# Building the two exponential tables of a 64-channel half jointly, in one tile

## The chip, the cores and the metric

The kernel runs on one core of one Trainium2 chip. The metric is the device time of one execution in microseconds (us), as the median of several runs on the same chip. A profile is one traced execution; its times count from the start of the span.

## The reference, cut to what matters

The program is four residual layers over x of 2048 x 512: A, B, A, B. Layer A is a state-space convolution, layer B a local dilated attention (not touched by the change).

```python
# layer A, on the layer-normalised input u (2048 x 512), D = 512 channels, N = 128 modes
dt = exp(log_dt)
P  = exp(dt * (A_re + 1j*A_im) [:, :, None] * l)      # D x N x 2048
K  = einsum("dn,dnl,dn->dl", Cc, P, dt*Bc).real       # the convolution kernel, D x 2048
y  = irfft(rfft(pad(u)) * rfft(pad(K)))[:2048] + u * Dskip
# ...
x = x + A(layernorm(x)); x = x + B(layernorm(x)); x = x + A(layernorm(x)); x = x + B(layernorm(x))
```

K depends on the parameters only, so the kernel builds it once, in its first stage, mixed with the first convolution. That stage is where the change lies.

## The kernel before

P at position l = 64*e + i is a product of a table X over e (32 entries) and a table Y over i (64 entries). The kernel works in eight halves of 64 channels. For each half DVE (VectorE) fills X and Y by doubling (entries m to 2m are entries 0 to m times a power), then makes three quarter products; PE (TensorE) contracts X with Y over the modes; ACT (ScalarE) evacuates the sum into KTq; a DMA takes it to DRAM and another fetches it in another layout as KT.

```python
def double(self, T, m, lev, hc):                       # before
    for e0 in range(0, m, HALF):                       # HALF = 8: pieces of at most 1024 columns
        mm = min(m, HALF)
        ta, tb = ...                                   # two scratch tiles
        nc.vector.tensor_tensor(v(ta), src, self.mult(self.MA, lev, hc, mm), ALU.mult)
        nc.vector.tensor_tensor(v(tb), src, self.mult(self.MB, lev, hc, mm), ALU.mult)
        nc.vector.tensor_tensor(T[..., m + e0:m + e0 + mm, :], ta, tb[:, ::-1], ALU.add)
# y_products: 3 x (Y quarter, Y2 quarter), each one tensor_tensor of 2048 columns
# contract: 256 small matmuls psk <- X, Y and psk <- X, Y2, then
        self.KTq = self.wk.tile([128, 1024], BF, name="KTq", tag="KTq")   # a buffer of its own
        nc.scalar.copy(KTq..., psk...)
        nc.sync.dma_start(self.kscr[hc]..., KTq...)
```

The first stage in program order. The input's FFT (`u_fft`), the kernel's spectrum (`k_fft`) and `finish` (spectral products, inverse, residual, write of X) are issued between tables and contraction.

```python
def half(hc, between=None):
    Xt, Y, Y2 = T.build(hc)
    T.x_part(Xt, hc); T.y_base(Y, hc); T.y_products(Y, Y2, hc)     # (half 0: y_base first)
    r = between() if between is not None else None     # u_fft(dc + 1) or k_fft(dc - 1)
    with tc.high_priority():
        T.contract(Xt, Y, Y2, hc)
    return r

for dc in range(4):                                    # a pair of halves = 128 channels
    Xr = residual(dc - 1) if dc > 0 else None
    Kt = half(dc * 2, (lambda: k_fft(dc - 1)) if dc > 0 else None)
    if dc > 0:
        cv.finish(dc - 1, xcs.pop(dc - 1), Kt, Xr)
    if dc < 3:
        half(dc * 2 + 1, mid)                          # mid: xcs[dc + 1] = cv.u_fft(dc + 1)
# ... half 7 in two parts, k_fft and finish of the last pair
```

`u_fft` and `k_fft` go matmuls (PE) - Z (ACT) - transposes (PE) - zt copy (DVE for the input, ACT for the kernel) - matmuls (PE) - xc or Kt (ACT). `finish` goes pa, pb (DVE) - inverse matmuls (PE) - VT (ACT) - matmuls with the residual Xr (PE) - X (ACT).

Of the kernel before, what the change touches and what calls it, by code (L numbers as in the profile page):

```python
# [19 lines left out]
D = 512  # L20
# [67 lines left out]

def make_consts(nc, const, C):
    fc = _fft_consts()  # L90
    bones_np = np.zeros((128, 4, 32), dtype=np.float32)
    for f in range(128):
        for k in range(4):
            bones_np[f, k, 8 * k + f // 16] = 1.0
    for name in ("F1", "F1T"):
        C[name + "_h"] = nc.inline_tensor(_bf(fc[name]), name="c_" + name)
    todo = [("ident", _bf(np.eye(128)), BF), ("C2", _bf(fc["C2"]), BF), ("IC", _bf(fc["IC"]), BF),
            ("bones", _bf(bones_np), BF), ("onesr", _bf(np.ones((1, 128))), BF)]
    for i, (name, arr, dt) in enumerate(todo):
        h = nc.inline_tensor(arr, name="c_" + name)  # L100
        t = const.tile(list(arr.shape), dt, name="sb_" + name)
        nc.sync.dma_start(t[:], h.ap())
        C[name] = t
# [32 lines left out]
class LnStats:  # L136


    def __init__(self, nc, pool, parts, nm, eps):
        self.nc, self.parts, self.eps = nc, parts, eps  # L140
        self.st = pool.tile([128, NJ, len(parts), 6], F32, name="ln_st_" + nm)
        self.mv = pool.tile([128, NJ, 2], F32, name="ln_mv_" + nm)
        self.den = pool.tile([128, NJ], BF, name="ln_den_" + nm)
        self.rstd = pool.tile([128, NJ], F32, name="ln_rstd_" + nm)
        self.nb = pool.tile([128, NJ], F32, name="ln_nb_" + nm)
# [208 lines left out]
def ladder(nc, pp, pst, identf, raw, MA, MB, cb, nu, fill):  # L354
# [27 lines left out]
    quad = pp.tile([128, 4, 4, NM], F32, name="quad")  # L382
    nc.vector.tensor_tensor(quad[:, :, 0, :], e[:], cs[:], ALU.mult)
    nc.vector.tensor_tensor(quad[:, :, 1, :], e[:], sn[:], ALU.mult)
    LAM = pp.tile([128, 2, D], F32, name="LAM0")
# [10 lines left out]
    def coefs():  # L396
# [12 lines left out]
        for q in (2, 3):  # L409
            pt = pst.tile([128, 4, NM], F32, name="ptq", tag="ptq")  # L410
            for t in range(4):
                nc.tensor.transpose(pt[:, t, :], quad[:, t, q, :], identf[:])
            nc.scalar.copy(cb[:, :, q - 2, :], pt[:].rearrange("n t (h d) -> n (t h) d", h=2))

    def multipliers(i, cur):

        src = cur[:].rearrange("n c (h d) -> n c h d", h=8)
        if i == "nu":
            nc.scalar.copy(nu[:, :, 0, :], src[:, 0])
            nc.scalar.activation(nu[:, :, 1, :], src[:, 1], ACT.Copy, scale=-1.0)  # L420
            return
        nc.scalar.copy(MA[:, i], src[:, 0].unsqueeze(2).to_broadcast([128, 8, 2, 64]))
        conj = 7 <= i <= 10
        nc.scalar.activation(MB[:, i, :, 0, :], src[:, 1], ACT.Copy, scale=-1.0 if conj else 1.0)
        nc.scalar.activation(MB[:, i, :, 1, :], src[:, 1], ACT.Copy, scale=1.0 if conj else -1.0)
# [3 lines left out]
    for i in range(11):  # L429
# [6 lines left out]
        multipliers(i if i != 6 else "nu", cur)  # L436
# [4 lines left out]
        if i == 5:  # L441
            l48 = pp.tile([128, 2, D], F32, name="l48")
            q1 = pp.tile([128, 2, D], F32, name="q1")
            q2 = pp.tile([128, 2, D], F32, name="q2")
            nc.vector.tensor_tensor(q1[:], l16[:], cur[:, 0:1, :].to_broadcast([128, 2, D]), ALU.mult)
            nc.vector.tensor_tensor(q2[:], l16[:], cur[:, 1:2, :].to_broadcast([128, 2, D]), ALU.mult)
            nc.vector.tensor_tensor(l48[:, 0, :], q1[:, 0, :], q2[:, 1, :], ALU.subtract)
            nc.vector.tensor_tensor(l48[:, 1, :], q1[:, 1, :], q2[:, 0, :], ALU.add)
            multipliers(LV48, l48)
# [5 lines left out]
class Tables:  # L455


    def __init__(self, nc, tc, es, MA, MB, cb, nu, psum, kscr):
        self.nc, self.MA, self.MB, self.cb, self.nu, self.ps, self.kscr = nc, MA, MB, cb, nu, psum, kscr
        self.tx = es.enter_context(tc.tile_pool(name="t_x", bufs=2))  # L460
# [3 lines left out]
    def mult(self, M, lev, hc, n):  # L464
        return (M[:, lev, hc].rearrange("n c (h t) -> n (c h) t", t=2).unsqueeze(2)
                .to_broadcast([128, 2 * HD, n, 2]))

    def double(self, T, m, lev, hc):

        nc = self.nc  # L470
        for e0 in range(0, m, HALF):
            mm = min(m, HALF)
            ta = self.wk.tile([128, 2, HD, HALF * 2], BF, name="ta", tag="ta")
            tb = self.wk.tile([128, 2, HD, HALF * 2], BF, name="tb", tag="tb")

            def v(t):
                return t[:].rearrange("n c h (e t) -> n (c h) e t", t=2)[:, :, 0:mm, :]
            src = T[:, :, :, e0:e0 + mm, :].rearrange("n c h e t -> n (c h) e t")
            nc.vector.tensor_tensor(v(ta), src, self.mult(self.MA, lev, hc, mm), ALU.mult)  # L479
            nc.vector.tensor_tensor(v(tb), src, self.mult(self.MB, lev, hc, mm), ALU.mult)  # L480
            nc.vector.tensor_tensor(T[:, :, :, m + e0:m + e0 + mm, :].rearrange("n c h e t -> n c h (e t)"),  # L481
                                    ta[:, :, :, 0:mm * 2], tb[:, ::-1, :, 0:mm * 2], ALU.add)

    def build(self, hc):
        nc = self.nc
        Y = self.ty.tile([128, 2, HD, EY, 2], BF, name="Ytab", tag="Ytab")
        Y2 = self.ty.tile([128, 2, HD, EY - EYB, 2], BF, name="Y2tab", tag="Y2tab")
        X = self.tx.tile([128, 2, HD, EX, 2], BF, name="Xtab", tag="Xtab")
        return X, Y, Y2

    def x_part(self, X, hc):
        nc = self.nc
        nc.gpsimd.memset(X[:, 0, :, 0, :], 1.0)
        nc.gpsimd.memset(X[:, 1, :, 0, :], 0.0)
        nc.vector.tensor_copy(X[:, :, :, 1, :].rearrange("n c h t -> n (c h) t"),
                              self.nu[:, hc].rearrange("n c (h t) -> n (c h) t", t=2))
        for lev in range(1, 5):
            self.double(X, 1 << lev, 6 + lev, hc)

    def y_base(self, Y, hc):  # L500
        self.nc.vector.tensor_copy(Y[:, :, :, 0, :].rearrange("n c h t -> n (c h) t"),
                                   self.cb[:, hc].rearrange("n c (h t) -> n (c h) t", t=2))
        for lev in range(4):
            self.double(Y, 1 << lev, lev, hc)

    def y_products(self, Y, Y2, hc, h0=0, h1=HD):

        nc = self.nc
        if h1 - h0 == HD:
            views = [(lambda t: t.rearrange("n c h e t -> n (c h) e t"), lambda m: m)]  # L510
        else:
            views = [(lambda t, c=c: t[:, c, h0:h1], lambda m, c=c: m[:, c * HD + h0:c * HD + h1]) for c in range(2)]
        for q, lev in ((1, 4), (2, 5), (3, LV48)):
            for v, vm in views:
                src = v(Y[:, :, :, 0:EYB, :])
                nc.vector.tensor_tensor(v(Y[:, :, :, q * EYB:(q + 1) * EYB, :]), src,  # L516
                                        vm(self.mult(self.MA, lev, hc, EYB)), ALU.mult)
                nc.vector.tensor_tensor(v(Y2[:, :, :, (q - 1) * EYB:q * EYB, :]), src,  # L518
                                        vm(self.mult(self.MB, lev, hc, EYB)), ALU.mult)

    def contract(self, X, Y, Y2, hc, half=None):
# [6 lines left out]
        for ds in range(n):  # L528
            for m in range(4):
                for g in range(4):  # L530
                    d = d0 + g * n + ds
                    h, t = d // 2, d % 2
                    xs = X[:, m // 2, h, :, t]
                    if m % 2 == 0:
                        nc.tensor.matmul(psk[32 * g:32 * g + 32, ds, :], xs, Y[:, m // 2, h, :, t],  # L535
                                         start=(m == 0), stop=False, skip_group_check=True)
                    else:
                        nc.tensor.matmul(psk[32 * g:32 * g + 32, ds, EYB:], xs, Y2[:, 1 - m // 2, h, :, t],  # L538
                                         start=False, stop=(m == 3), skip_group_check=True)
        if half != 1:  # L540
            self.KTq = self.wk.tile([128, 1024], BF, name="KTq", tag="KTq")
# [10 lines left out]
def kernel_and_first_conv(nc, tc, C, prm, x2d, const, kt_dram, kscr, ln, ln_b):  # L552
    with ExitStack() as es:
        mt = es.enter_context(tc.tile_pool(name="k_mt", bufs=1))
        MA = mt.tile([128, 11, 8, 2, 64], BF, name="MA")
        MB = mt.tile([128, 11, 8, 2, 64], BF, name="MB")
        cb = mt.tile([128, 8, 2, 64], BF, name="cb")
        nu = mt.tile([128, 8, 2, 64], BF, name="nu")
        psk = es.enter_context(tc.tile_pool(name="k_psk", bufs=1, space=PSUM))
        T = Tables(nc, tc, es, MA, MB, cb, nu, psk, kscr)  # L560
        with tc.tile_pool(name="k_prep", bufs=1) as pp, tc.tile_pool(name="k_pst", bufs=2, space=PSUM) as pst:
# [6 lines left out]
            Drow = mt.tile([1, D], BF, name="Drow")  # L568
            nc.sync.dma_start(Drow[:], prm["Dskip"].rearrange("(o d) -> o d", o=1))
# [10 lines left out]
            ladder(nc, pp, pst, identf, raw, MA, MB, cb, nu, fill)  # L580
        psT = es.enter_context(tc.tile_pool(name="k_psT", bufs=2, space=PSUM))
        psA = es.enter_context(tc.tile_pool(name="k_psA", bufs=2, space=PSUM))
        cv = Conv(nc, tc, es, C, X, psA, psT, ("zt_xc",))
# [3 lines left out]
        def half(hc, between=None):  # L587
            Xt, Y, Y2 = T.build(hc)
# [462 lines left out]
```

## Time and profile before

| | before |
|---|---|
| median, range (us) | 609.28 (609.2 to 611.79) |
| profiled span, mean granted TensorE clock | 606.0 us, 0.918 |
| last table product ends | 233.9 us |
| first X write of finish(0), (1), (2) | 127.2, 175.4, 225.4 us |
| first copy of the attention stage (xnT) | 266.3 us |

The page's list of busy time by engine, before (busy us, share of the span, number of instructions):

```profile
PE 445.1 (73%) x5743; PEld 289.0 (48%) x5786; DVE 514.4 (85%) x976; ACT 338.9 (56%) x465; POOL 12.7 (2%) x50
```

The view by windows, before (window, its length, then busy us and instructions of PE, PEld, DVE, ACT and POOL, then granted clock, DMA share and GB/s; PEld is PE's weight load):

```profile
195.00:245.00 50.00, 36.73 (x817) 27.16 (x820) 48.31 (x101) 29.30 (x38) 1.14 (x1) 0.88 0.20 55
```

DVE is busy 48.3 of 50 us: the stage runs at DVE's pace, and stays so up to 245 us. The groups by form, before, from 38 to 240 us (number, then total busy us and mean ns of one, then idle time before them), here one of the two groups of quarter products:

```profile
L516 DVE TENSOR_TENSOR Ytab<-Ytab,MA 128x2048 bf16<-128x2048 bf16 x21 | 25.6, 1220 | 0.2
```

### The profile page before, as it was taken

To read this page: it belongs to the slowest core of one execution; us is meant where nothing else is said; L and a number is where in the kernel's file an instruction comes from. 1 tells how busy PE (TensorE), PEld (TensorE's weight loads), DVE (VectorE), ACT (ScalarE), POOL (GpSimd) and SP (SyncE) were. 2 spreads that over 40 slices of the span, in tenths; PEclk is the share of its full clock that TensorE was granted. 3 is DMA by queue.
4 is the path that set the end of the run, shared out by engine and by line. 5 is a ranking of instruction groups with operands and counts; after the bars stand their busy time and mean duration, and the time that the engine had idled before them with its cause. 6 is when DMAs were issued, how large, how long until landed. Compare 5 with 4: busy or idle time off the path is not lost.

```text
span 606.0 us, 13365 instructions
## 1 busy us (share of the span) xinstructions
PE 445.1 (73%) x5743; PEld 289.0 (48%) x5786; DVE 514.4 (85%) x976; ACT 338.9 (56%) x465; POOL 12.7 (2%) x50
## 2 busy tenths in 40 slices
PE   1101776876767776679987779978995899858996
PEld 0100554564554565454332766656764433327763
DVE  5999799998998999775977899859999588689950
ACT  4999357555662755646574223467973556722144
POOL 0000000000000000400000000000000000000000
PEclk9999989898996897869998599989998799968999
DMA  9101001221131023600004060000000000040011
GB/s 291 67 1 35 19 20 37 87 56 36 41 103 37 3 106 72 209 1 1 2 1 118 4 264 16 2 0 1 3 1 0 2 2 0 1 121 1 1 72 69
DMA packets 24346, 28.78 MB, mean 47 GB/s; under 512 B 15074, under 2 KB 20067, under 8 KB 23007
## 3 DMA queue, kind: packets, MB, share of 16 engines
q1 hardware_dynamic: 22702, 27.54, 13.8%
q8 instruction: 45, 0.74, 0.5%
q10 hardware_dynamic: 1584, 0.39, 0.3%
q14 instruction: 15, 0.11, 0.1%
HBM read 15.89 MB, written 8.39 MB: 40 GB/s over the span
## 4 chain that ended last, share of the span: by engine, by line
DVE 52%; PE 28%; ACT 9%; issue 8%; DMA 2%; POOL 0%; SPq 0%; POOLq 0%; ACTq 0%; DVEq 0%
PE ps_qk L829 7%; DVE prod L931 6%; DVE ta L479 4%; DVE Y2tab L518 4%; DVE tb L480 4%; DVE Ytab L516 4%; PE ps_o L955 4%; PE ps_v L843 3%; DVE Xtab L481 3%; DVE ln_st_b L150 3%; PE Lp L875 2%; DVE Ytab L481 2%; PE po L946 2%; DVE ln_st_a L150 2%; DVE pa L726 2%
## 5 line engine op out<-in xcount | busy, mean ns | idle before, releaser
L946 PE MATMUL po<-sb_ident,prod 128*128 128x128 bf16 x1024 | 72.7, 232 | 11.4 <-DVE prod L931 7.9
L946 PEld LDWEIGHTS <-prod 128*128 128x128 bf16 x1024 | 65.2, 105 | 20.6 <-DVE prod L931 17.2
L829 PE MATMUL ps_qk<-xnT,wqk 128*128 128x512 bf16 x245 | 63.7, 391 | 4.3 <-ACT xnT L814 1.2
L862 DVE TENSOR_TENSOR prod<-qT,kT 128x2048 bf16<-128x2048 bf16 (+3 forms) x48 | 43.2, 953 | 14.0 <-ACT qT L831 7.2
L931 DVE TENSOR_TENSOR prod<-V,L 128x2048 bf16<-128x2048 bf16 (+3 forms) x48 | 43.6, 947 | 6.4 <-PE po L946 6.4
L949 ACT CAST oT<-po 128x1024 bf16<-128x1024 f32 x16 | 15.4, 1015 | 56.6 <-PE po L946 56.6
L195 PE MATMUL psA<-X,sb_F 128*128 128x128 bf16 x128 | 14.9, 236 | 36.2 <-ACT X L578 32.3
L870 DVE TENSOR_TENSOR prod<-qT,kT 128x2048 bf16<-128x2048 bf16 (+3 forms) x40 | 34.9, 902 | 6.9 <-ACT kT L831 4.3
L829 PEld LDWEIGHTS <-wqk 128*128 128x128 bf16 x256 | 23.5, 100 | 32.5 <-issue 12.2
L195 PEld LDWEIGHTS <-sb_F 128*128 128x128 bf16 x256 | 16.6, 100 | 45.6 <-issue 42.8
L535 PE MATMUL psk<-Ytab,Xtab 128*32 128x64 bf16 x1024 | 26.1, 214 | 15.6 <-DVE Xtab L481 5.8
L955 PE MATMUL ps_o<-wo_t,oT 128*128 128x512 bf16 x121 | 33.5, 380 | 4.7 <-ACT oT L949 3.9
L931 DVE TENSOR_TENSOR prod<-Vp,L 128x2048 bf16<-128x2048 bf16 (+3 forms) x40 | 34.9, 896 | 0.0
L182 ACT CAST Z<-psA 128x1024 bf16<-128x1024 f32 (+1 forms) x32 | 28.8, 974 | 9.6 <-PE psA L195 9.5
L875 PE MATMUL Lp<-prod,sb_bones 128*32 128x512 bf16 x256 | 25.4, 416 | 9.6 <-DVE prod L870 4.9
L538 PE MATMUL psk<-Y2tab,Xtab 128*32 128x48 bf16 x1024 | 24.8, 211 | 9.8 <-issue 7.3
L535 PEld LDWEIGHTS <-Xtab 128*32 128x32 bf16 x1024 | 22.7, 113 | 17.9 <-issue 15.2
L516 DVE TENSOR_TENSOR Ytab<-Ytab,MA 128x2048 bf16<-128x2048 bf16 (+1 forms) x33 | 30.6, 929 | 0.2
L518 DVE TENSOR_TENSOR Y2tab<-Ytab,MB 128x2048 bf16<-128x2048 bf16 (+1 forms) x33 | 30.6, 927 | 0.0
L843 PE MATMUL ps_v<-wv,xnT 128*128 128x512 bf16 x126 | 28.2, 379 | 1.8 <-ACT V L845 1.7
L538 PEld LDWEIGHTS <-Xtab 128*32 128x32 bf16 x1024 | 22.2, 106 | 13.0 <-issue 11.8
L150 DVE BATCH_NORM_STATS2 ln_st_b<-X 128x6 f32<-128x384 bf16 (+2 forms) x80 | 23.5, 357 | 3.8 <-ACT X L308 3.8
(195 smaller groups left out, 1100.0 us busy)
## 6 DMA issues: line engine op xcount, KB each, us to landing
kt_scratch<-Kt SPq DMA_DIRECT2D x4, 1024.0 KB, 4.3
Kt<-kt_scratch SPq DMA_DIRECT2D x4, 1024.0 KB, 7.2
Vp<-V SPq DMA_DIRECT2D x2, 1568.0 KB, 9.1
X<-in_A_u_dram SPq DMA_DIRECT2D x4, 512.0 KB, 5.6
Xr<-in_A_u_dram SPq DMA_DIRECT2D x4, 512.0 KB, 4.6
out_dram<-X SPq DMA_DIRECT2D x4, 512.0 KB, 2.6
k_scratch<-KTq SPq DMA_DIRECT2D x7, 256.0 KB, 2.0
KT<-k_scratch SPq DMA_DIRECT2D x7, 256.0 KB, 3.5
```

The lines of the kernel that those rows point to most:

```text
L150: self.nc.vector.bn_stats(self.st[:, j, part, :], X[:, j, a:b])
L516: nc.vector.tensor_tensor(v(Y[:, :, :, q * EYB:(q + 1) * EYB, :]), src, vm(self.mult(self.MA, lev, hc, EYB)), ALU.mult)
L518: nc.vector.tensor_tensor(v(Y2[:, :, :, (q - 1) * EYB:q * EYB, :]), src, vm(self.mult(self.MB, lev, hc, EYB)), ALU.mult)
L535: nc.tensor.matmul(psk[32 * g:32 * g + 32, ds, :], xs, Y[:, m // 2, h, :, t], start=(m == 0), stop=False, skip_group_check=True)
L538: nc.tensor.matmul(psk[32 * g:32 * g + 32, ds, EYB:], xs, Y2[:, 1 - m // 2, h, :, t], start=False, stop=(m == 3), skip_group_check=True)
L829: nc.tensor.matmul(ps[:], wqk[:, ct, f0:f0 + 128], xnT[:, ct, s0:s0 + 512], start=(ct == 0), stop=(ct == 3))
L843: nc.tensor.matmul(ps[:].rearrange("p a b -> p (a b)"), xnT[:, ct, j * 128:(j + 1) * 128], wv[:, ct, :], start=(ct == 0), stop=(ct == 3))
L862: nc.vector.tensor_tensor(pr[:, :, (ja - j0) * 128:(ja - j0) * 128 + n], qT[fp][:, :, ja * 128: ja * 128 + n], kT[fp][:, :, (ja - sh) * 12 ...
L875: nc.tensor.matmul(Lp[r0:r0 + 32, w // 4, :], bones[:, w % 4, :], pr[:, f2, hb * 512:(hb + 1) * 512], start=(w % 4 == 0), stop=(w % 4 == 3 ...
L931: nc.vector.tensor_tensor(p2[:, ja - j0: ja - j0 + n, :].rearrange("p j (t d h) -> p (j t) d h", t=2, d=DH), src.rearrange("p j (t d h) -> ...
L946: nc.tensor.matmul(po[f2][:, jj, :], p2[:, jj, f2 * 128:(f2 + 1) * 128], ident[:], start=(w == 0 and jj % 4 == 0), stop=(w == W - 1), skip ...
L955: nc.tensor.matmul(ps[:], oT[:, ft, j * 128:(j + 1) * 128], wo_t[:, ft, :], start=(ft == 0), stop=False)
```

## The change

Its intent: less fixed cost on DVE. X's first 16 entries and Y's base become neighbours in one tile and are doubled together; the first product is written in place and the second added to it; two or three quarter products become one instruction; a contraction matmul reads both Y parts in one operand. The larger tiles need SBUF, so three buffers are given up: KTq moves into the two zt buffers of the FFT, Z loses its second buffer, and the residual Xr shares KT's buffer. Constants of later stages move out of the first stage's pools, so the attention weights are loaded at a different moment.

```diff
-        for e0 in range(0, m, HALF):
-            ... ta = src * MA; tb = src * MB; T[m:2m] = ta + swapped tb      # X and Y each
+        for lev in range(4):                                # x0:x1 = both bases
+            nc.vector.tensor_tensor(dst, src, mult(0), ALU.mult)
+            nc.vector.tensor_tensor(tb[...], src, mult(1), ALU.mult)
+            nc.vector.tensor_tensor(d, d, tb[..., ::-1, ...], ALU.add)
+        # then high(): X entries 16 to 31, three passes of 2048 columns
+        # y_products: one of 2048, one of 4096, one of 6144 columns instead of six of 2048
 ...
-            self.KTq = self.wk.tile([128, 1024], BF, name="KTq", tag="KTq")
+            self.KTq = self.kq.tile([128, 1024], BF, name="KTq", tag="zt")
 ...
-        cv = Conv(nc, tc, es, C, X, psA, psT, ("zt_xc",))
+        cv = Conv(nc, tc, es, C, X, psA, psT, ("zt_xc",), zbufs=1)
+        T.kq = cv.w
 ...
-                cv.finish(dc - 1, xcs.pop(dc - 1), Kt, Xr)
+                cv.finish(dc - 1, xcs.pop(dc - 1), Kt, residual(dc - 1, kp, "KT"))
 ... (multiplier layout, matmul operands, placement of constants: cut)
```

## The prediction

> **What bounds the kernel now.** The page's busy list gives DVE 514 of 606 us (85%), PE 445, ACT 339. The change lies in the first stage (0 to about 264 us: ladder, tables, first convolution). The table by windows shows DVE busy 44 to 48 of each 50 us from 60 to 260, and the waits view finds about 14 us of DVE idle in 38 to 265. One pair of halves takes 48.3 us on DVE (start of products 109.7 to 158.0 in the timeline), with about 1.2 us idle. So DVE bounds this stage; PE and ACT follow closely.
>
> **What the change removes.** The groups by form sum to 171.6 us of table work (doublings 106.8, products 61.2, copies 3.6). The timeline, start to start: a doubling level costs three passes at 2 elements per cycle plus about 0.45 us (256 columns 0.86, 512 1.25, 1024 2.05); independent products 1.14 per 2048 columns, of which only about 0.07 is fixed. The Trainium skill, "VectorE: DVE Perf Modes", perf-mode tier table, caps bf16 tensor_tensor at 2x, 1224 ns for 2048; the trace has 1220. So merging saves fixed costs, not elements.
> - Old half: X 8.25, Y 4.96, products 6.82, copies 0.24: 20.3 us.
> - New half (estimate): joint base 0.86+1.25+2.05+3.65=7.8, high level 3.65, products 6.6, copy 0.1: 18.2 us.
>
> That is 2.1 us less for six halves, about 0.2 for half 0, about 2.6 for half 7: 15 us of DVE. The joined operands leave the matmuls' number and size.
>
> **What it adds.** ACT's multipliers become four 512-column copies a level (0.53 start to start) in place of 0.93+0.53+0.53: about 2.5 us more in the ladder. KTq moves into the two zt buffers, Z has one buffer, the residual shares KT's. The instruction order shows KTq's evacuation moved behind the third block of the FFT before it, so the kernel spectrum and its k_scratch round trip (2.0 + 3.5 us) start later, and finish(2) moves behind half 7's products. The attention weights' load, and the wv copies (3.05 us on the chain at 252), move ahead of the tail: up to 3 us back.
>
> **How much is on the path.** PE's serial work for one pair, summed from the timeline: two contractions 8.8, finish 11.2, input FFT 12.2, kernel FFT 11.7: 44 us. DVE falls from 48.3 to 44.2. So PE/ACT becomes co-critical at once: I expect 45 to 46 us a pair, and PE enters the tail one kernel FFT (about 12 us) behind, which costs back much of what the pairs gain.
>
> **Predicted: 604 us**, 8 in 10 between 595 and 612. Faster by over 2%: 0.20; within 2%: 0.74; slower by over 2%: 0.06.
>
> **What would show it right.** DVE busy down 15 to 20 us; 2048-column doublings near 1.22 us, the 6144-column product near 3.3; last table product at about 215 instead of 233.8; new DVE waits of over 10 us in all, for PE or for Kt, at 205 to 245; later stages (264 on) unchanged within 1 us; matmul durations unchanged.
>
> **What would make it wrong.** If PE's chain is shorter than my sum (its idle hides DVE's lateness), the pairs keep 4 us each and the end lands near 595. If KTq's shared buffer stalls the FFTs, or the one-piece 2 to 3.3 us products hold zt copies and PE behind them, it is slower than before. If an in-place or reversed operand ran at 1x, DVE would grow instead.

## More of the kernel before

The order of each engine's instructions is fixed when the program is built: the kernel's framework decides it from the program order, the priorities and its own model of when operands are ready.

Now the beats of the stage on ACT. The timeline of ACT before (start, duration, source line, what, and in brackets the idle time ahead and what ended it, as far as the profile names it):

```profile
92.15 1.01 ACT L544 CAST KTq<-psk 128x1024 bf16<-128x1024 f32 x1 [6.52 <-issue]
...
127.17 1.01 ACT L308 CAST X<-psA 128x1024 bf16<-128x1024 f32 x1 [1.57 <-remote]
...
175.44 1.01 ACT L308 CAST X<-psA 128x1024 bf16<-128x1024 f32 x1 [1.57 <-remote]
...
225.40 1.01 ACT L308 CAST X<-psA 128x1024 bf16<-128x1024 f32 x1 [1.57 <-remote]
...
266.27 1.01 ACT L814 COPY xnT<-pt_x 128x1024 bf16<-128x1024 bf16 x1 [1.44 <-PE pt_x L809]
```

And PE around the first kernel spectrum, k_fft(0), before. Lines with psA<-KT are the first step of the spectrum, psk is a contraction:

```profile
98.56 0.23 PE L195 MATMUL psA<-KT,sb_F 128*128 128x128 bf16 x1 [0.20 <-DMA KT<-k_scratch]
...
98.88 1.19 PE L195 MATMUL psA<-KT,sb_F 128*128 128x128 bf16 x15
100.54 0.61 PE L195 MATMUL psA<-KT,sb_F 128*128 128x128 bf16 x8 [0.48 <-ACT Z L182]
...
109.71 0.38 PE L224 MATMUL psA<-zt,sb_C 128*128 128x512 bf16 x1
110.02 0.21 PE L538 MATMUL psk<-Y2tab,Xtab 128*32 128x48 bf16 x4
...
114.00 0.23 PE L538 MATMUL psk<-Y2tab,Xtab 128*32 128x48 bf16 x2 [2.02 <-issue]
```

The last 252 matmuls of half 2's contraction (the first four go ahead singly) follow 44 of the 48 transposes and matmuls of the spectrum's second step: they delay the last quarter of it only. "issue" in the last line is a wait for nothing that the profile shows.

`with tc.high_priority(): contract` is in both kernels and is not touched.

## The result, and the profile after

| | before | after |
|---|---|---|
| median, range (us) | 609.28 (609.2 to 611.79) | 627.05 (623.59 to 630.68) |
| profiled span, mean granted clock | 606.0, 0.918 | 621.8, 0.898 |
| last table product ends | 233.9 | 217.1 |
| first X write of finish(0), (1), (2) | 127.2, 175.4, 225.4 | 142.0, 193.8, 240.0 |
| first xnT | 266.3 | 281.7 |

All outputs are right. The ratio is 1.0292 (95% interval 1.0243 to 1.0341): slower by over 2%. Here and below a ratio is the mean time of one kernel's fast runs over that of the other's of the same rounds, so not quite the ratio of the medians quoted.

```profile
PE 455.7 (73%) x5786; PEld 293.2 (47%) x5786; DVE 504.4 (81%) x851; ACT 340.6 (55%) x478; POOL 12.6 (2%) x50
```

That is the page's busy list after: DVE works 10 us less. The groups by form after show the merged operations at the expected rate:

```profile
L545 DVE TENSOR_TENSOR Y2tab<-Ttab,MPB 128x6144 bf16<-128x6144 bf16 x7 | 23.5, 3350 | 0.0
L545 DVE TENSOR_TENSOR Ttab<-Ttab,MPA 128x4096 bf16<-128x4096 bf16 x7 | 16.0, 2284 | 0.0
```

The view by windows after:

```profile
195.00:245.00 50.00, 33.73 (x663) 24.54 (x662) 30.94 (x50) 32.29 (x38) 6.06 (x1) 0.93 0.37 113
```

DVE is through with its tables 16.8 us earlier (233.9 - 217.1) and then idles: 31 of 50 us busy where it was 48. Yet the stage ends 15.4 us later (281.7 - 266.3), which is all but 0.4 us of the span's 15.8. The later stages are unchanged; the loss is in the chain that is not DVE's tables. ACT's timeline after:

```profile
100.19 1.01 ACT L573 CAST KTq<-psk 128x1024 bf16<-128x1024 f32 x1 [0.40 <-PE psA L228]
...
142.01 1.01 ACT L312 CAST X<-psA 128x1024 bf16<-128x1024 f32 x1 [1.57 <-PE psA L310]
...
193.80 1.01 ACT L312 CAST X<-psA 128x1024 bf16<-128x1024 f32 x1 [1.57 <-PE psA L310]
...
239.98 1.01 ACT L312 CAST X<-psA 128x1024 bf16<-128x1024 f32 x1 [1.57 <-PE psA L310]
...
281.69 1.01 ACT L849 COPY xnT<-pt_x 128x1024 bf16<-128x1024 bf16 x1 [1.99 <-PE pt_x L844]
```

Finish(0) is 14.8 us late, and most of the loss is there already. PE's timeline after, from u_fft(1)'s transposes (pt) over k_fft(0) to finish(0) (L249 to L252 are the inverse's matmuls), shows how:

```profile
89.94 1.07 PE L214 MATMUL pt<-sb_ident,Z 128*128 128x128 bf16 x16
94.31 0.59 PE L225 MATMUL psA<-zt,sb_C 128*128 128x512 bf16 x1 [3.31 <-DVE zt L184]
...
104.63 0.21 PE L563 MATMUL psk<-Ttab 128*32 128x64 bf16 x4 [3.52 <-DVE Ttab L545]
106.13 0.27 PE L199 MATMUL psA<-KT,sb_F 128*128 128x128 bf16 x1 [1.28 <-DMA KT<-k_scratch]
...
106.54 1.78 PE L199 MATMUL psA<-KT,sb_F 128*128 128x128 bf16 x15
108.25 0.23 PE L566 MATMUL psk<-Y2tab,Ttab 128*32 128x48 bf16 x4
...
112.89 0.26 PE L566 MATMUL psk<-Y2tab,Ttab 128*32 128x48 bf16 x2
113.08 1.89 PE L199 MATMUL psA<-KT,sb_F 128*128 128x128 bf16 x16
...
128.41 0.27 PE L252 MATMUL psA<-sb_IC,pa 128*128 128x256 bf16 x1
128.62 0.21 PE L566 MATMUL psk<-Y2tab,Ttab 128*32 128x48 bf16 x4
...
132.69 0.20 PE L566 MATMUL psk<-Y2tab,Ttab 128*32 128x48 bf16 x3 [2.39 <-issue]
...
133.48 0.39 PE L249 MATMUL psA<-sb_IC,pa 128*128 128x256 bf16 x1
```

The contraction of half 2 now stands in the middle of the spectrum's first step (108.25 to 113.08, 4.8 us), and the contraction of half 3 in the middle of finish(0)'s inverse (128.62 to 133.48, 4.9 us). Before, the first stood near the end of the spectrum's second step and the second behind finish(0). The 14.8 us are then, by these lines: the spectrum starts 7.6 us later (106.1 against 98.6), and what it waits for last is the fetch of KT, since KTq was evacuated 8.0 us later (100.19 against 92.15); two blocks of 4.8 and 4.9 us inside the chain, against one of 4.5 (110.0 to 114.5) before. That sums to 12.8 of the 14.8. Of the two blocks 1.5 and 2.4 us are holes in which PE waits for nothing that the profile shows; the one before has such a hole too, of 2.0 us.

The late KTq is only the last of the waits before the spectrum. Half 1's contraction, which ends at 89.8 us, stands ahead of u_fft(1)'s transposes (89.94), and these are followed by a wait of 3.31 us for DVE's zt copy, so PE has u_fft(1) done at 101.1 us only. Run e4 below, with KTq evacuated early, starts its spectrum no sooner than that.

At the end of the stage, the chain of waits after (start, us, what):

```profile
228.54 4.08 ACT wv L873 x4
...
241.05 0.23 PE psA L310
...
241.29 2.72 DMA KT<-k_scratch
...
251.28 0.59 ACT KTq L573
...
251.89 2.58 DMA k_scratch<-KTq
...
254.60 2.20 DMA KTu<-k_scratch
```

Four copies of attention weights (wv) lie on it, a fetch of KT into the buffer that the residual held until then (L310 reads the residual, the fetch follows), and half 7's first KTq with its two DMAs.

### The profile page after: what moved, and what is told of

Read it like the earlier page. It is cut to its first block, busy times and chain, and to the rows that moved or that the text cites. A ratio compares the mean times of both kernels' runs of the same rounds, so it can differ in the third digit from the quotient of the medians.

```text
span 621.8 us, 13330 instructions
## 1 busy us (share of the span) xinstructions
PE 455.7 (73%) x5786; PEld 293.2 (47%) x5786; DVE 504.4 (81%) x851; ACT 340.6 (55%) x478; POOL 12.6 (2%) x50
## 4 chain that ended last, share of the span: by engine, by line
PE 26%; DVE 21%; ACT 9%; issue 7%; DMA 1%; POOL 0%; POOLq 0%; ACTq 0%; SPq 0%
PE ps_qk L864 7%; DVE prod L966 6%; PE ps_o L990 4%; PE ps_v L878 3%; PE Lp L910 2%; PE pt_x L844 2%; PE po L981 2%; DVE pa L761 1%; DVE pb L762 1%; DVE prod L905 1%; DVE VT L784 1%; DVE zt L743 1%; DVE ln_st_b L154 1%; PE ps_o L992 1%; ACT oT L984 1%
## 5 line engine op out<-in xcount | busy, mean ns | idle before, releaser
L864 PE MATMUL ps_qk<-xnT,wqk 128*128 128x512 bf16 x256 | 65.5, 392 | 3.1 <-ACT xnT L849 2.3
L984 ACT CAST oT<-po 128x1024 bf16<-128x1024 f32 x16 | 15.4, 1015 | 56.6 <-PE po L981 56.6
L199 PEld LDWEIGHTS <-sb_F 128*128 128x128 bf16 x256 | 19.8, 114 | 49.7 <-issue 44.5
L279 ACT CAST VT<-psA 128x512 bf16<-128x512 f32 x31 | 16.6, 597 | 30.1 <-PE psA L252 20.7
L186 ACT CAST xc<-psA 128x1024 bf16<-128x1024 f32 x16 | 15.9, 1017 | 30.5 <-PE psA L228 30.5
L563 PE MATMUL psk<-Ttab 128*32 128x64 bf16 x1024 | 23.7, 207 | 11.8 <-issue 4.3
L566 PE MATMUL psk<-Y2tab,Ttab 128*32 128x48 bf16 x1024 | 23.0, 203 | 11.2 <-issue 11.2
L214 PE MATMUL pt<-sb_ident,Z 128*128 128x128 bf16 x240 | 23.1, 263 | 7.5 <-ACT Z L186 7.5
L563 PEld LDWEIGHTS <-Ttab 128*32 128x32 bf16 x1024 | 20.5, 106 | 16.5 <-issue 15.7
```

What stands on the lines that cost most here:

```text
L186: self.nc.scalar.copy(dst, src)
L199: nc.tensor.matmul(o, F1[:, j, r, :], rhs_j(j), start=True, stop=not dk)
L563: nc.tensor.matmul(o.rearrange("e (s i) -> e s i", s=2), xs, T[:, 1:3, h, m // 2, :, t], start=(m == 0), stop=False, skip_group_check=True)
L864: nc.tensor.matmul(ps[:], wqk[:, ct, f0:f0 + 128], xnT[:, ct, s0:s0 + 512], start=(ct == 0), stop=(ct == 3))
```

## The experiments

Theories at the start. K: the shared KTq buffer delays KTq and with it the spectrum. X: the residual in KT's buffer delays the fetch. Z: the single Z buffer stalls the FFTs. After the first four runs there were added P: the contraction blocks on PE stand before the FFT and finish work, now that DVE is no longer later than that; S: the PE and ACT chain is simply that long behind DVE's longer pieces; W: the wv copies. Times are medians; after the ratio to before stands its 95% interval; the last two columns are from each run's trace. All had three rounds; each had its own runs of before (medians 607.9 to 608.8).

| run | edit | time (us) | ratio to before | X of finish(0), (1), (2) | xnT |
|---|---|---|---|---|---|
| e1 | before, KTq in the zt buffers | 619.71 | 1.0192 (1.0168 to 1.0216) | 135.0, 193.9, 237.8 | 277.8 |
| e2 | before, one Z | 609.72 | 1.0023 (1.0004 to 1.0041) | 128.4, 176.7, 225.7 | 268.1 |
| e3 | after, KTq on its own | 623.03 | 1.0239 (1.0217 to 1.0261) | 138.2, 190.8, 242.4 | 281.5 |
| e4 | e3, residual on its own | 616.79 | 1.0132 (1.0115 to 1.015) | 138.3, 188.4, 241.6 | 274.0 |
| e5 | e4, no priority | 606.80 | 0.9964 (0.9931 to 0.9997) | 127.2, 173.2, 223.3 | 264.2 |
| e6 | before, no priority | 609.28 | 1.0008 (0.997 to 1.0045) | 132.7, 180.4, 228.1 | 268.2 |
| e7 | e5, wv on POOL | 599.38 | 0.9859 (0.9836 to 0.9883) | 127.1, 173.0, 223.1 | 254.6 |
| e8 | after, no priority | 609.02 | 1.0003 (0.997 to 1.0037) | 128.2, 172.8, 219.8 | 268.7 |
| e9 | before, wv on POOL | 609.35 | 1.002 (0.9983 to 1.0058) | 128.4, 177.8, 226.3 | 268.4 |
| e10 | e1, no priority | 610.88 | 1.0056 (1.0035 to 1.0078) | 132.1, 181.1, 228.9 | 270.4 |
| e11 | e8, wv on POOL | 605.53 | 0.9966 (0.9924 to 1.0007) | 127.4, 172.2, 217.9 | 263.3 |
| e12 | e7, zt copies on ACT | 593.63 | 0.977 (0.9747 to 0.9794) | 123.8, 169.2, 219.4 | 251.2 |
| e13 | after, wv on POOL | 624.93 | 1.0283 (1.0223 to 1.0343) | 143.3, 194.0, 240.9 | 281.5 |
| e14 | before, e12's three edits | 605.93 | 0.9946 (0.9926 to 0.9967) | 129.8, 178.0, 227.0 | 263.6 |

### The buffers: e1 to e4

```diff
# e1, on before
-            self.KTq = self.wk.tile([128, 1024], BF, name="KTq", tag="KTq")
+            self.KTq = self.kq.tile([128, 1024], BF, name="KTq", tag="zt")
+        T.kq = cv.w
# e2, on before
-        cv = Conv(nc, tc, es, C, X, psA, psT, ("zt_xc",))
+        cv = Conv(nc, tc, es, C, X, psA, psT, ("zt_xc",), zbufs=1)
# e3, on after: one table tile of five slots (quarter products 2 and 3 shared by successive halves),
# which frees 8 KB per partition (that it leaves PE's order alone is on record before the run; no run shows it), and then
-            self.KTq = self.kq.tile([128, 1024], BF, name="KTq", tag="zt")
+            self.KTq = self.wk.tile([128, 1024], BF, name="KTq", tag="KTq")
# e4, on e3
-    residual(dc - 1, kp, "KT")
+    residual(dc - 1, kp, "Xr")
```

> The kernel before with one part of the change: KTq takes a buffer of the two that the FFT blocks (zt) rotate through. Theory K (the shared KTq buffer delays KTq's evacuation and with it the spectrum chain): slower by 12 to 20 us, 620 to 630 us, with the last X write of the first stage at 272 to 282 us instead of 264 and last table product still near 234. Rival Z (the single Z buffer) and rival T (the reshaped table work itself): within 3 us of before.

> The kernel before with one part of the change: one Z buffer instead of two. Theory K: within 3 us of before (the order of PE's instructions does not change at all). Rival Z: slower by 5 us or more.

> The changed kernel with KTq in a buffer of its own again; room for it is made by sharing the third slot of the table tile between the two halves (5 slots instead of 2 x 3), which alone leaves PE's order as it was. Theory K: the loss is gone, 595 to 606 us; DVE work as in the changed kernel. Rival T: stays at 620 or more.

> As the run before, and the residual tile gets its own buffer again instead of that of KT. Theory K with Xr as a second, smaller part: 2 to 3 us less than the run before, since the fetch of KT for half 6 no longer waits for the last use of the residual. If Xr does not matter: the same within 1 us.

e1 lost 1.9%, just under what theory K said; e2 shows that the single Z costs next to nothing in before, and e5 and e8 keep it without a loss, so Z falls. But e3, which undoes what e1 did, stayed at 623 where K had expected 595 to 606: a miss. e4 gained 6 us more, twice what was expected. With all of the suspected buffers undone but Z, the changed tables were still 1.3% slower than before, though their DVE was through 18 us earlier (last product at 215.8 us). The first X of finish(0) came no more than 3.8 us earlier than in after, in e3 and in e4. Yet both evacuate half 1's KTq as early as before does (92.09 and 91.53 us). e4's ACT and then its PE:

```profile
91.53 1.01 ACT L579 CAST KTq<-psk 128x1024 bf16<-128x1024 f32 x1 [4.51 <-issue]
```

```profile
101.98 0.22 PE L199 MATMUL psA<-KT,sb_F 128*128 128x128 bf16 x1
```

With KTq early the spectrum still starts at 102.0 (in e3 103.0), right behind u_fft(1), which half 1's contraction holds up here too. So of the 7.6 us by which it is late in after, 3 to 4 go with the late KTq. PE's timeline of e4 also showed the contraction of half 3 standing inside finish(0), behind five of its last matmuls and before the others:

```profile
131.34 0.44 PE L308 MATMUL psA<-VT,sb_F1T 128*128 128x128 bf16 x5 [1.16 <-ACT VT L279]
131.71 0.21 PE L572 MATMUL psk<-Y2tab,Ttab 128*32 128x48 bf16 x4
...
136.22 0.22 PE L572 MATMUL psk<-Y2tab,Ttab 128*32 128x48 bf16 x4
136.37 0.34 PE L308 MATMUL psA<-VT,sb_F1T 128*128 128x128 bf16 x3
```

4.7 us (131.71 to 136.37) stand between two parts of one group. From this came theory P.

### The order on PE: e5, e6, e8, e10

```diff
# the same edit on e4 (e5), before (e6), after (e8), e1 (e10): halves 0 to 6; half 7 keeps its priority
-            with tc.high_priority():
-                T.contract(Tt, Y2, hc)
+            T.contract(Tt, Y2, hc)
```

> The changed tables with KTq and the residual in buffers of their own (run e4, 616.8 us), and the high priority taken from the contractions of halves 0 to 6. In the order of PE's instructions the last 252 matmuls of a contraction then no longer stand as one block inside the kernel's spectrum (k_fft) and inside finish, but go in pieces between the steps. Theory P (in e4 that block stood on PE before work of the FFT and finish chain: 109.2 to 113.4 us inside k_fft(0), 131.7 to 136.3 us inside finish(0), each about 4.5 us of the chain): first X of finish(0) at 128 to 132 us instead of 138.3, the first X to X period 46 us or less instead of 50.1, total 600 to 608 us. Theory S (the chain over PE and ACT is simply that long, and zt copies and products wait behind the longer pieces of DVE): X of finish(0) at 136 us or later, total 613 to 620 us.

> Control: the kernel before, with the high priority taken from the contractions of halves 0 to 6 likewise. Theory P and S alike: DVE is what before waits for, and its contraction blocks already stood behind the FFT's turns, so within 4 us of before (605 to 612 us). If it gets faster by 5 us or more, what e5 wins is not the change's own loss but something open to both kernels.

> The changed kernel itself (KTq and the residual in shared buffers as they are), with the high priority taken from the contractions of halves 0 to 6. Theory P: the preemption costs it 5 to 10 us, the shared buffers the rest: 616 to 622 us. If the shared buffers alone make the loss, it stays at 625 to 629 us.

> Run e1 (before with KTq in the zt buffers, 619.7 us) with the high priority taken from the contractions of halves 0 to 6. Theory P: most of e1's 11 us came from the order that the shared buffer gave the contractions on PE (blocks inside the spectrum and inside finish), not from the wait for the buffer itself: 608 to 613 us. Theory K (the wait for the buffer itself is the cost): 617 to 621 us.

e5 met the three numbers of theory P or went just past them: X of finish(0) at 127.2 (128 to 132 expected), the next 46.0 us later, 606.8 us in all; S falls. e6 takes as long as before (1.0008, interval 0.997 to 1.0045), though X of finish(0) comes 5.5 us later in it. And e8, which is the changed kernel with nothing undone but the priority of the contractions, gained more than P had said (609.0 us, where 616 to 622 were expected): its ratio went from 1.0292 to 1.0003, a difference as large as the whole measured loss. The timelines of PE and then of ACT in e8, to be compared with those of after:

```profile
96.89 0.27 PE L199 MATMUL psA<-KT,sb_F 128*128 128x128 bf16 x1 [5.92 <-DMA KT<-k_scratch]
...
97.31 1.78 PE L199 MATMUL psA<-KT,sb_F 128*128 128x128 bf16 x15
100.58 1.89 PE L199 MATMUL psA<-KT,sb_F 128*128 128x128 bf16 x16
```

```profile
91.05 1.01 ACT L573 CAST KTq<-psk 128x1024 bf16<-128x1024 f32 x1 [0.87 <-PE psk L566]
...
128.20 1.01 ACT L312 CAST X<-psA 128x1024 bf16<-128x1024 f32 x1 [1.57 <-remote]
...
172.84 1.01 ACT L312 CAST X<-psA 128x1024 bf16<-128x1024 f32 x1 [1.57 <-remote]
...
219.77 1.01 ACT L312 CAST X<-psA 128x1024 bf16<-128x1024 f32 x1 [1.57 <-remote]
```

The two parts of the spectrum's first step are 3.3 us apart (97.31 to 100.58) instead of 6.5 (106.54 to 113.08), KTq is evacuated at 91.05 instead of 100.19 with the very same shared buffer, and the pairs take 44.6 and 46.9 us (172.84 - 128.20, 219.77 - 172.84) instead of 51.8 and 46.2. u_fft(1)'s transposes start at 80.48 instead of 89.94. DVE is busy for 43.9 of the 44.6 us of the first pair, so DVE may well set the pace again there. From X of finish(2) to xnT, however, e8 takes 48.9 us, against 40.9 in before and 41.7 in after: what the pairs gained is given back in the tail. There ACT waits 3.97 us for the load of wv and then copies for 4.15 us (from 226.07), and DVE waits 9.8 us for Kt.

The edit is single, but it changes more than the two blocks: the order on DVE and ACT changes with it, and the holes inside the contractions are gone (15.5 us of them on PE from 60 to 265 us in after, none in e8). Taking away 7.6 us of holes in before (12.6 to 5.0 in e6) gained nothing.

e10 tells what e1 had measured: without the priority the shared KTq costs 0.56% instead of 1.92%. Most of e1's loss goes with the priority. PE's order in e1's program had changed: the contraction of half 3 stood inside finish(0)'s last matmuls there, and behind finish(0) in before. So a buffer's sharing can cost through the order that the framework then chooses, more than through the wait for the buffer.

### The weight copies and the zt copies: e7, e9, e11, e13, e12, e14

```diff
# e7 on e5, e9 on before, e11 on e8, e13 on after
-                nc.scalar.copy(wv[...], wvn[...])
+                nc.gpsimd.tensor_copy(wv[...], wvn[...])
# e12 on e7; e14: before with this, the wv edit and no priority
-        cv = Conv(nc, tc, es, C, X, psA, psT, ("zt_xc",), ...)
+        cv = Conv(nc, tc, es, C, X, psA, psT, (), ...)
```

> e5 with the four copies of the weights wv moved from ACT to POOL. Theory W (in after the four copies, 4.1 us of ACT, stood ahead of finish(2)'s VT evacuations, on the chain): 2 to 4 us less than e5, if in e5 they still stand on the chain. If the copies cost nothing where e5 puts them: within 1.5 us of e5.

> Control: the kernel before, with nothing but the four copies of the weights wv moved from ACT to POOL. In before they ran at 252.4 us, 3.05 us of ACT ahead of the last VT evacuations. Theory W (they lie on the chain there too): 2 to 5 us less than before, 603 to 606 us, so that a part of e7's gain is open to both kernels. If they did not lie on the chain of before: within 1.5 us of before.

> The changed kernel as it is (shared buffers) without the priority (run e8, 609.0 us), and the wv copies on POOL. Theory W: 3 to 8 us less than e8, 601 to 606 us; the sharing of the buffers then costs 2 to 6 us against e7 (599.4 us), most of it in the tail, where the contraction of half 7 is evacuated at 236 us.

> The changed kernel as it is, high priority and shared buffers included, with nothing but the wv copies moved from ACT to POOL. Its trace had the four copies, 4.08 us, on the chain ahead of finish(2)'s VT evacuations, so theory W says 3 to 5 us less than the changed kernel (ratio to before 1.021 to 1.025, 621 to 624 us). If contraction blocks on PE hide it (theory P alone): within 1.5 us of the changed kernel, ratio 1.027 or more.

e13 is a miss for theory W: the four copies, 4.08 us on the chain of after, were taken away and the ratio stayed (1.0283 against 1.0292). In its trace finish(2)'s VT evacuations then wait for PE instead, and X of finish(2) comes at 240.9, not earlier than the 240.0 of after. e9 is a miss too: before gained nothing. Where the contraction blocks are gone, however, the same edit is worth more than expected: 7.4 us from e5 to e7 (1.05 points of ratio). Its size has a reason in e5's timeline of ACT:

```profile
226.26 1.11 ACT L878 COPY wv<-wvn 128x512 bf16<-128x512 bf16 x1 [1.94 <-DMA wvn<-in_B_wqkv_dram]
227.28 1.00 ACT L312 CAST X<-psA 128x1024 bf16<-128x1024 f32 x1
```

ACT stood 1.94 us for the load of the weights, with the second X write behind it: X at 227.28, in e7 at 224.47, and 4.5 us of copies (four of 1.11 to 1.15) lie among the X and Z evacuations that follow. 1.94 + 4.5 = 6.4 of the 7.4 us. From e8 to e11 the same edit gave 3.5 us of median, with intervals that overlap (0.997 to 1.0037, 0.9924 to 1.0007), so that one is unclear.

> e7 (599.4 us) with the zt copies of the input's FFT moved from DVE to ACT too: 16 copies of 0.6 us, about 10 us of DVE, against some 16 us of ACT in pieces of 1.0 us. If DVE's tables still lead the stage: the last table product 6 to 10 us earlier than 217.7 us and the total 593 to 598 us. If the chain over PE and ACT leads now: each turn 0.4 us slower, 599 to 606 us.

> Control for e12 (593.6 us): the kernel before with its old tables and the same three edits of the schedule (no high priority for the contractions of halves 0 to 6, wv copies on POOL, zt copies on ACT). If the changed tables are what gains once the schedule lets them: this one stays at 599 us or more, so e12 is ahead by 5 us or more. If the schedule's edits alone make the gain: 592 to 596 us.

e12 beats both kernels: 593.63 us (592.87 to 594.9), 2.3% under before, as expected where DVE leads (593 to 598). The last table product came at 214.0 instead of 217.7 us, less than the 6 to 10 expected, so only a part of the 10 us taken from DVE came through; the rest is again chain. The old tables with the same three edits (e14) reach 0.9946. The two runs had different rounds, so the comparison is by ratios: 0.977 / 0.9946 = 0.982, so the changed tables gain about 1.8% once the schedule lets them.

The granted clock differs a little with the runs (0.898 after, 0.913 in e8, 0.918 before), but does not order them: e4 had 0.922 and was 1.3% slower than before, e10 had 0.907 at 0.6%.

## Why the prediction was wrong

Point by point:

- **DVE's side: right, with a smaller busy figure.** The last table product was to come at about 215 and came at 217.1; the 6144-column product took 3.35 us (3.3 predicted), the 2048-column ones 1.22. DVE busy fell 10.0 us, not 15 to 20. One term was mis-sized: the lowest joint level was put at 0.86 us and its three passes measure 0.38, 0.38 and 0.40 us each (estimate, from the group's means: 0.3 us a half more, some 2.4 us for eight halves; the rest of the gap is not accounted for).
- **Later stages unchanged, matmul durations unchanged: right.** The stage's end carries 15.4 of the 15.8 us. Contraction matmuls took 207 and 203 ns on average against 214 and 211.
- **"New DVE waits of over 10 us in all, for PE or for Kt, at 205 to 245": right in kind, short in size.** The waits view from 38 to 290 us after has this line (us in all, times, longest):

```profile
DVE pa L269 <- ACT Kt L186: 13.3, 6, 6.0
```

  Of these 6.5 us lie between 205 and 245, 11.1 up to 262; before has 0.5 in all.

- **The step that failed: "So PE/ACT becomes co-critical at once: I expect 45 to 46 us a pair".** The sum treats PE's work as a plain total of 44 us and asks nothing about where each part stands. The contractions are issued at high priority; in after they stand ahead of u_fft(1)'s transposes, inside the spectrum and inside finish, the last two as blocks of 4.8 and 4.9 us that PE works through before it goes on with the chain. In place of 45 to 46 us the runs showed a chain 14.8 us late before the first full pair began, then pairs of 51.8 and 46.2. Without the priority the same tables lose nothing against before (e8: 1.0003, interval 0.997 to 1.0037), and before itself does not change without it (e6: 1.0008). Whether the sum of 44 us was sound is not shown: pairs take 44.6 to 46.9 us in e5 and e8 (but for e5's last, 50.1, where both parts of half 7's contraction, which kept its priority, stand inside finish(2)), but DVE, predicted at 44.2, is busy for 98% of e8's first pair and can set that pace just as well.
- **"PE enters the tail one kernel FFT (about 12 us) behind": the size fits by luck.** X of finish(2) came 14.6 us late (240.0 against 225.4), but 14.8 of that was there at finish(0). The prediction had the pairs' gain pay for most of the lag; in after there was no such gain. In e8 there was, and the tail took it back; so without the priority the outcome is the predicted one, 609.0 us against 595 to 612, though the wv copies and the shared buffers are part of that tail (e11, e5).
- **"Up to 3 us back" from the wv copies: wrong place.** They came on the chain at 228.5 (4.08 us) instead. They did not matter there either (e13); they do in the mended schedule (e7), and so the early load costs time there instead of giving it back.
- **"If KTq's shared buffer stalls the FFTs ... it is slower": named as a risk, under-weighted, and only half of it.** The late KTq was seen in the instruction order before the run. Its 8.0 us in the trace go with the priority too (e8: 91.05 us with the same buffer), and undoing it alone brought finish(0) forward by 3.8 us only (e3). Under the priority the two buffers are worth 1.6 points of ratio together (1.0292 to 1.0132, e4), so the priority and the buffers are not separate shares of the loss. In the mended schedule the shared KTq and residual together cost 0.4 points of ratio (e8 to e5, intervals overlap) without the wv edit and 1.1 with it (e11 to e7).
- **"... or the one-piece 2 to 3.3 us products hold zt copies and PE behind them": small.** PE's waits for DVE's zt copies sum to 5.9 us before and 6.5 after, from 60 to 245 us; the longest, 3.31 us in u_fft(1), is gone in e8.
- **Not foreseen:** the fetch of KT waiting for the residual's buffer; e4 puts the residual's sharing at 6 us under the priority.

What stays open: why the order changes as it does inside the framework was not tested, only its effect; 2 of finish(0)'s 14.8 us; and the split of the loss in after between the late u_fft(1), the two blocks, the holes inside them and the new order on DVE and ACT, since the one edit changes them all.

## What to carry to other kernels

When an engine that paces a stage gets faster, ask which work moves forward with it and whose way it then stands in: a high priority that was harmless in one program can, in the next, put a block of work ahead of the chain that paces the stage next. Compare each engine's instruction order, not only the busy sums, and test the order by undoing the priority alone: that one edit brought 1.0292 to 1.0003, while undoing two of the buffers brought 1.0132. A cause seen on the chain (here the wv copies) may be worth nothing until the longer one is gone, so re-try such edits after each step.

## What the Trainium skill lacked or had wrong

- "Runtime: NRT & Kernel Launch", section "Instruction fetch mechanics", says that an engine's instructions are refilled in blocks of 256 (16 KiB) and that the cost of a boundary is "mostly hidden". In the runs here a contraction sent as one block (256 matmuls and 256 weight loads) mostly has a hole with nothing that the profile shows: 7 holes, 15.5 us in all from 60 to 265 us after (no contraction matmul's record is missing in these traces), 7 holes and 12.6 us before, 5 holes and 5.0 us in e6 (5 and 6.1 in e10, 4 and 6.0 in e14), and none in e5, e7, e8, e11 and e12, where the contractions are spread. Whether these holes are instruction fetch no run here shows; the page gives no size of such a stall to compare.
- "VectorE: DVE Perf Modes", section "The perf-mode tier table (the rule you actually need)", gives tensor_tensor in bf16 2x, 1224 ns for 2048 columns. The trace agrees (1217 to 1225 ns). For the lowest level (one entry doubled) it is not the whole rule: 256 columns took 378 to 400 ns there, and 285 to 294 ns at a level of two entries before. The page has nothing on how the operand's shape costs this; what it is in the shape was not tested.
- None of the pages read treats the order in which an engine's work is issued as a cost that depends on another engine's speed: the same priority cost nothing in before (e6, 1.0008) and 2.9% in the changed kernel (1.0292 to 1.0003).
